# Sums of v in the value tiles of the first group, and its raw x kept as two parts

## The chip, the cores and the metric

The kernel runs on one core of one Trainium2 chip. The metric is the device time of one execution in microseconds (us). The engines are TensorE (PE, its weight loads PEld), VectorE (DVE), ScalarE (ACT), GpSimd (POOL) and SyncE (SP); SP issues all the transfers (DMA) of this program.

## The reference

The input is q, k and v of 4 batches, 8 heads, 768 positions and 64 features. Each position attends to the keys closer than 16 and, besides, to 24 summaries, one for each block of 32 positions. The output of the attention goes through a feed-forward layer with softplus.

```python
k_sum = k.reshape(B, H, nb, block, D).max(axis=3)
v_sum = v.reshape(B, H, nb, block, D).mean(axis=3)
scores_l = scale * np.matmul(q, k.transpose(0, 1, 3, 2))
scores_s = scale * np.einsum('bhsd,bhnd->bhsn', q, k_sum) + np.log(block)
scores_all = np.concatenate([np.where(mask_l, scores_l, -1e9), scores_s], axis=-1)
...
v_all = np.concatenate([v, v_sum], axis=2)
attn = np.matmul(a, v_all)            # a: softmax of scores_all
...
h = x @ w_in                          # x: attn, heads side by side, 3072 x 512
g = np.maximum(h, 0.0) + np.log1p(np.exp(-np.abs(h)))
return g @ w_out                      # 512 x 2048 and 2048 x 512
```

## The kernel before

The 3072 tokens are 12 chunks of 256, and two chunks make a group: x = 0 to 5. A window is 64 queries with 96 keys (KW) and the 24 summaries behind them, so 120 in all (KS). The attention of one chunk works on two head pairs (hp, hp + 1) at once: a block. Each group thus has four blocks, (chunk 0 or 1) by (head pairs 0, 1 or 2, 3).

The feed-forward layer is done twice over: for each group the first half of the 16 slices of the hidden layer, then, from the last group back to group 0, the second half. The second half needs x once more, in another form (a Strassen-like scheme with sums and differences of the four blocks). For that the raw blocks r (128 x 512) of groups 0 to 4 are stored to DRAM at the start (`keep`, DRAM tiles `raw`) and loaded back in the last phases (`attended`). The order of all instructions is a list of task numbers, SEQUENCE, written out in the file; every engine runs its tasks in that order, and so does SP with its DMAs. A tile with `bufs=1` is only written again when its readers are done.

Every x is held as two parts in the PE's rounded format: `xw[:, part 0]` is the rounded value (`high`, L786 on ACT) and part 1 the rest (`low`, L790 on DVE).

Group 0 is treated apart, since the program starts with it:

- `FirstPlaces` puts its queries and values into tiles named `first` (one for each head pair). A value tile has 96 rows for each window; the rows 96 to 119 stay unused.
- `declare_first_values` computes the 24 sums of v on the PE (L430, into `vt`); ACT scales them into `v0` (L441, `mean`), in the rows 96 to 119 of its tile.
- `attention` has the scores on the PE (L646, `sc`), the mask on DVE (L659), the exponential on ACT (L667), the transposes on the PE (L700, `pt`), their copies on ACT (L704, `pT`), and then `values` (L746 and L754, `xo`): 16 matmuls with 96 rows for each block, and for the sums 4 more with 24 rows and 256 columns that add to the same `xo`.
- After that, `take` copies `xo` into a raw block r (L767: two of the four on ACT, two on DVE), which `keep` stores.

In all other groups the sums lie in the rows 96 to 119 of the value tile itself (a DMA spreads them, L545, `v<-vs`), and a value matmul has 120 rows.

Of the kernel before, what the change touches and what calls it, by code (L numbers as in the profile page):

```python
# [10 lines left out]
F32 = mybir.dt.float32  # L11
# [136 lines left out]
23 124 0 125 2 3 25 4 44 47 5 134 161 6 7 24 8 31 27 9 10 126 130 35 11 127 12 128 13 129 14 26 131 33 50 1 132 133a  # L148
51 15 16 52 17 85 18 135 136 66 19 137 20 138 29 21 22 45 82 162 139 37 163 166 53 32 164 54b 165 39 41 67 167 34 284
48 143 68 36 28 55 30 140 57 88 46 168 69 38 49 89 70 40 56 58 90 104 86 180 169 42 84 141a 105 142a 43 106 291 91 59  # L150
309 148a 92a 144 145 146 83 87 147 152 107 170 71 61 108 171 63 62 73 72 292 74 75 334 338 293 149 64 60a 181 93 182
95 183 316 77 79 184 94 96 97 351 76 80 150a 185 120 199 78 294 295a 153a 109 157 154 111 155 110 156 112 113 296 317
158 101 99 100 176 102 151a 159 218 336 115 117 160a 318 297 342 340 116 227 346 98a 118 186 285 121 335 219 339 228
172 173 174 220 319 358 221 229 222 230 223 376 289 337a 114 320b 234 235 224 175 344 286 204 231 177 298 301 299 290
321 241 343 236 287 300 242 187 237 178 341a 225 243 244 226 179 232 288 322 345 359 189 360 233 123 122 239 190 238
245 347 200a 188 302 310 361 383 201 362b 323 348 314 202 240 248 203 468b 472a 205 363 312 313 249 246 303 469b 467
384 326 324 191a 385 325 315 311 255 195a 206a 192 207 364 208 209 256 193 386 194 247 250 251 257 475 252 196 258 327
494b 259 387b 498a 262 349a 365 368 366 263 352 355 328 350 493 356 197a 269 388 367 198a 210a 270 476 353 357 354 495
253 264 211 389 65 643 265 212 214 213 254 271 266 501 272 215 273 369 519 477 260 377 380 216a 217 378 381 261 520a
478 526 521b 390 393 267 370 307 479a 305 308a 306a 372 392 391 382 480 268 373a 329 379 274 502 481 641 278 645 503  # L160
276 330a 332a 333a 277 275 529 394 547 331 548a 549 374a 375 395 399 482 485 484 470 279 397a 398 400 401 402 504 473
483 103 471 474 505 410 403 404 554a 281 282 405 644 506 411 406 412 413 530 507 407 649 647 408 414 409 531 557 486
659a 660b 417 532 533a 418 534 508 509 415 419 648 558 487a 420 510 511 496 500 658 653 304 497 416 421 499 559 655
535 422 642 650 646 665 651 652 424 560 425 561a 426 668 686 427 428 512 513 522 525 536 81 431 438 432 423 429 430
562 669 524 539 537 527 654 517 670 518a 489a 687 693a 523 528 538 563 439 433 440 434 435 441 442 688b 436 671 672b
696 715a 714 119 540 541a 491a 545 550 556 564 566 543a 492a 490a 673 697 719 716 567 552 565 445 446 447 448 437 443
449 656 553 551 555 698 444 396 371 674 450 544 722 741a 742a 699 700a 568 452 569 675 661 573 574 453 515 571a 280
572a 701 546a 516a 575 454 455 283 663 740 745a 576 451 577 578 456 458 488 723 457 459 678 676 657 460 461a 584 585
464a 890 462 724 579 662 580 702 667 677 591 725 726 748 570 586 581 727 833b 582 894 592 587 588 598 749 839 832 664
# [41 lines left out]
1763 1767 1765a 1611 1901 1623 1768 1615 1676 1769a 1677 1678 1620 1616 1679 1680 1682 1685 1770a 1681 1683 1621 1687  # L211
1689 1617 1686 1688 1777a 1766a 1895 1691 1618 1692 1667 1690 1684 1696 1693 1624 1697 1668 1669 1698 1701 1704 1625
1702a 1670 1705 1707 1774a 1708 1712 1703 1713 1710 1706 1711 1714 1716 1674 1709 1715 1717 1721 1675 1898 1694 1780
1718 1905 1722 1723 1726 1622 1729 1727 1728 1735 1732 1730 1695 1737 1626 1731 1736 1778a 1772 1896 1699 1739 1779a
1897a 1733 1775 1781a 1740 1738 1734 1741 1742 1700 1719 1720 1724 1899a 1743 1782a 1773a 1746 1747 1748 1776 1783
1785 1786 1789 1784a 1787 1725 1790 1788 1794 1792 1791 1793 1902a 1795 1796 1757 1797 1744 1745 1798 1799 1800 1805
1806 1750 1807 1751 1810 1811 1758 1753 1755 1812 1819 1813 1820 1814 1749 1754 1756 1815 1752 1821 1816 1823 1817
1822 1818 1759 1825 1826 1908a 1824 1827 1830 1831 1801 1903 1802 1803 1832 1804 1808 1835 1841 1836a 1838 1837 1839
1840 1842 1844 1846 1843 1845 1847 1850 1809 1904 1848 1849 1828 1851 1852 1855 1829 1856 1857 1860 1863 1900a 1866
1862 1911 1861a 1864 1867 1871 1865 1869 1872 1870 1760 1909a 1912 1914a 1913a 1875 1876 1873 1906 1868 1833 1874  # L220
1910a 1877 1834 1915 1853 1880 1916a 1907a 1881 1882 1917 1920 1918a 1919 1923 1921 1928 1926 1922 1887 1891 1930 1854
# [10 lines left out]
def kernel(  # L232
# [9 lines left out]
    nc = tc.nc  # L242
# [233 lines left out]
    class Places:  # L476


        def __init__(self, c, hp, sums, pads, apart):
# [9 lines left out]
            self.apart, self.sums = apart, None  # L489
# [60 lines left out]
    class FirstPlaces:  # L550


        def __init__(self, hp, sums, own, sp):
# [27 lines left out]
            v_keys.append(sums.first_v)  # L581
            self.tiles = []
            for i in range(n_c):
# [4 lines left out]
                tiles.sums = lambda g: sums.first(hp + g)  # L588
# [33 lines left out]
    def attention(x, i, hp, tiles, by_pe):  # L622
# [117 lines left out]
        def values():  # L740
            apart = bool(tiles.sums)
            for g in range(NG):
                for w in range(NWIN):
                    v = tiles.v(g)[:KW if apart else KS, w]
                    for h in range(2):
                        nc.tensor.matmul(  # L746
                            xo()[h * D:(h + 1) * D, g * CH + w * QW:g * CH + (w + 1) * QW],
                            lhsT=v[:, h * D:(h + 1) * D], rhs=queries(g, w, h)[:KW if apart else KS],
                            start=not (apart and (g or w)), stop=not apart,
                        )  # L750
# [9 lines left out]
        order.add(PE, 1.6 if tiles.sums else 1.2, values, [pT, *((pT, k) for k in range(NSQ)), *tiles.v_keys], [xo])  # L760

        r = None
        if x < NX - 1:
            r = block(2 * i + hp // NG)

            def take(copy):
                copy(out=r(), in_=xo())  # L767
            order.add(
                ACT, act(NG * CH, True), lambda: take(nc.scalar.copy), [xo], [r],
                ways=[Way(DVE, dve(NG * CH), lambda: take(nc.vector.tensor_copy))],  # L770
            )
            if x:
                return r
# [18 lines left out]
        return r  # L792
# [509 lines left out]
    for hp in range(0, NHP, NG):  # L1302
# [94 lines left out]
```

## Time and profile before

| | us |
|---|---|
| median of 3 runs (614.16 to 617.19) | 614.34 |
| the profiled execution, its own time | 613.83 |
| its span, first to last instruction | 612.0 |
| PE busy in the span | 602.7 |
| DVE, ACT, POOL busy | 379.3, 343.3, 180.6 |
| granted PE clock, mean | 1.000 |

The rows of the next section are of the profiled execution, whose own time is 613.83 us: its span of 612.0 us and 1.8 us around it. PE is busy for 98% of the span; this is a mean over stages, and what sets the end in a stage is read from the waits of that stage. A line number is that of the kernel before.

### The profile page before, as it was taken

How to read it: one execution, taken by the hardware profiler on the slowest of the kernel's cores; microseconds unless marked ns; L12 is line 12 of the kernel's file. 1: busy time of each engine (PE TensorE's matmuls, PEld its weight loads, DVE VectorE, ACT ScalarE, POOL GpSimd, SP SyncE). 2: the span in 40 equal slices, each digit the busy share in tenths (PEclk: the TensorE clock that was granted, in tenths of full speed). 3: DMA queues.
4: the chain of work that ended last, by engine and by line, in shares of the span. 5: the costliest groups of instructions: out<-in, count | busy, mean ns of one | idle time of the engine just before them, and what ended most of it. 6: DMA issues, size and time to landing. Idle time of an engine off the chain costs nothing.

```text
span 612.0 us, 12214 instructions
## 1 busy us (share of the span) xinstructions
PE 602.7 (98%) x4575; PEld 505.6 (83%) x4575; DVE 379.3 (62%) x992; ACT 343.3 (56%) x846; POOL 180.6 (30%) x178
## 2 busy tenths in 40 slices
PE   8899999999999999999999999999999999999997
PEld 7567878888788888888888888899898989999996
DVE  4999987846465665442235689854765655554543
ACT  4989998986778656576266986432213222233211
POOL 4445255134115132210003553572411216012000
PEclk9999999999999999999999999999999999999999
DMA  8999778966868576665428520041040230020121
GB/s 304 310 314 250 236 238 258 280 193 230 263 196 263 175 213 225 213 201 193 135 75 270 206 70 1 1 155 52 2 172 2 103 138 1 35 103 1 48 92 69
DMA packets 66714, 96.13 MB, mean 157 GB/s; under 512 B 5888, under 2 KB 44896, under 8 KB 65888
## 3 DMA queue, kind: packets, MB, share of 16 engines
q1 hardware_dynamic: 66656, 95.36, 48.1%
q8 instruction: 36, 0.59, 0.4%
q14 instruction: 22, 0.18, 0.1%
HBM read 66.06 MB, written 27.26 MB: 152 GB/s over the span
## 4 chain that ended last, share of the span: by engine, by line
PE 86%; DVE 11%; ACT 2%; issue 1%; POOL 0%; DVEq 0%; ACTq 0%; POOLq 0%
PE po L1224 40%; PE ph L1059 21%; PE hx L1099 10%; PE hy L1099 7%; PE xo L746 4%; PE sc L646 3%; DVE sp L659 1%; PE warm L1298 1%; DVE t L948 1%; DVE t L940 1%; DVE ks L352 1%; DVE w L973 1%; DVE gl L1217 1%; DVE tb L713 1%; DVE t L944 1%
## 5 line engine op out<-in xcount | busy, mean ns | idle before, releaser
L1224 PE MATMUL po<-w,gh 128*128 128x512 f32 x766 | 202.7, 392 | 0.3 <-DVE w L973 0.3
L1224 PEld LDWEIGHTS po<-w,gh 128*128 128x128 f32 x766 | 141.0, 188 | 29.6 <-DVE w L973 0.7
L1059 PE MATMUL ph<-xw,w 128*128 128x512 f32 x672 | 161.9, 392 | 0.2 <-POOL w L973 0.2
L1059 PEld LDWEIGHTS ph<-xw,w 128*128 128x128 f32 x672 | 125.1, 188 | 28.1 <-POOL w L973 0.7
L1224 PE MATMUL po<-w,gl 128*128 128x512 f32 x383 | 114.5, 392 | 0.6 <-DVE gl L1217 0.6
L1224 PEld LDWEIGHTS po<-w,gl 128*128 128x128 f32 x383 | 70.7, 188 | 15.3 <-DVE gl L1217 1.0
L667 ACT ACTIVATE sp<-sp,nm 128x120 f32<-128x120 f32 x192 | 73.1, 384 | 5.9 <-DVE nm L659 5.7
L1209 ACT ACTIVATE gh<-hx 128x512 fp32r<-128x512 f32 x20 | 12.0, 600 | 107.6 <-DVE hx L1109 107.6
L962 POOL TENSOR_TENSOR t<-t,raw 128x1024 int32<-128x1024 int32 (+1 forms) x20 | 40.8, 2044 | 103.9 <-DVE t L948 70.0
L1217 DVE TENSOR_TENSOR gl<-ph,gh 128x512 fp32r<-128x512 f32 x56 | 38.2, 686 | 53.0 <-ACT ph L1213 52.8
L1209 ACT ACTIVATE gh<-ph 128x512 fp32r<-128x512 f32 x56 | 33.4, 598 | 37.7 <-PE ph L1059 37.3
L803 POOL TENSOR_TENSOR x<-r,x 128x512 fp32r<-128x512 f32 x23 | 30.5, 1339 | 67.9 <-DVE x L796 58.2
L659 DVE CUSTOM_DVE_ANT_0 sp<-sc,added 128x120 f32<-128x120 f32 x192 | 40.8, 278 | 5.9 <-PE sc L646 4.9
L667 ACT ACTIVATION_READ_ACCUMULATOR sp<-sp,nm 128x1 f32 x192 | 36.2, 189 | 0.0
L1099 PE MATMUL hx<-x,w 128*128 128x256 f32 x240 | 35.7, 285 | 0.0
L1099 PE MATMUL hx<-x,sw 128*128 128x256 f32 x240 | 35.5, 284 | 0.0
L1099 PEld LDWEIGHTS hx<-x,w 128*128 128x128 f32 x240 | 32.9, 190 | 2.1
L1099 PE MATMUL hy<-x,sw 128*128 128x256 f32 x240 | 34.4, 284 | 0.0
L1209 ACT ACT_TABLE_LOAD x23 | 29.5, 1283 | 6.3 <-PE ph L1059 5.9
L1213 ACT ACTIVATE ph<-ph 128x512 f32<-128x512 f32 x56 | 32.9, 591 | 0.0
L1099 PEld LDWEIGHTS hx<-x,sw 128*128 128x128 f32 x240 | 32.0, 190 | 0.8
L1099 PEld LDWEIGHTS hy<-x,sw 128*128 128x128 f32 x240 | 31.2, 191 | 0.2
(122 smaller groups left out, 828.0 us busy)
## 6 DMA issues: line engine op xcount, KB each, us to landing
squares<-tb SPq DMA_DIRECT2D x20, 512.0 KB
pT<-squares SPq DMA_DIRECT2D x80, 128.0 KB
raw<-w_out_dram SPq DMA_DIRECT2D x16, 512.0 KB
kf<-kT_dram SPq DMA_DIRECT2D x16, 384.0 KB
raw<-w_in_dram SPq DMA_DIRECT2D x6, 1024.0 KB
q<-qT_dram SPq DMA_DIRECT2D x20, 256.0 KB
raw<-r SPq DMA_DIRECT2D x20, 256.0 KB
part<-ob SPq DMA_DIRECT2D x10, 512.0 KB
```

What stands on the lines that cost most here:

```text
L646: nc.tensor.matmul(unit(g * NU + h * NPAIR + i)[r * QW:(r + 1) * QW, k0:k1], lhsT=q[rows, w * QW:(w + 1) * QW], rhs=k[rows], start=True, s ...
L659: nc.vector.tensor_tensor_reduce(out=sp()[:, n], in0=unit(n), in1=added()[:, kinds.index((lows[w], lows[w + 1]))], scale=-SCALE, scalar=FL ...
L667: nc.scalar.activation(sp()[:, n], sp()[:, n], AF.Exp, bias=nm()[:, n:n + 1], scale=-1.0, accum_out=ss()[:, n:n + 1],)
L746: nc.tensor.matmul(xo()[h * D:(h + 1) * D, g * CH + w * QW:g * CH + (w + 1) * QW], lhsT=v[:, h * D:(h + 1) * D], rhs=queries(g, w, h)[:KW ...
L803: engine.tensor_tensor(to(1), a(), to(0).bitcast(F32), op=ALU.subtract)
L962: nc.gpsimd.tensor_tensor(a, a, word(0, I32), op=ALU.add)
L1059: nc.tensor.matmul(ph(), lhsT=lhs(part, cc), rhs=xw[cc][0]()[:, xw[cc][1], a], start=cc == 0 and n == 0, stop=cc == NCC - 1 and n == 2,)
L1099: nc.tensor.matmul(to()[:, half], lhsT=lhs(wa, cc), rhs=of_x(xa)[:, cc * CH:(cc + 1) * CH], start=cc == 0 and m == 0, stop=cc == NG - 1 an ...
L1209: nc.scalar.activation(gh(), all_of(), AF.Softplus)
L1213: nc.scalar.activation(all_of(), all_of(), AF.Softplus)
L1217: nc.vector.tensor_sub(out=gl(), in0=all_of(), in1=gh().bitcast(F32))
L1224: nc.tensor.matmul((to or po[t])()[:, c0:c1], lhsT=a()[:, t * P:(t + 1) * P], rhs=w2()[:, part, i2 * DM + c0:i2 * DM + c1], start=(f == f0 ...
```

## The change

Three things change, all for group 0.

1. The sums of v go into the value tiles: four DMAs (L585 of the changed kernel, one for each head pair) copy the 24 rows of `v0` into the rows 96 to 119 of the `first` tile, once for each of its 8 windows, 96 KiB a DMA. The value matmuls then have 120 rows, and the 4 matmuls for the sums of each block are gone.
2. The raw block r of group 0 is no longer copied out of `xo` and stored. In its place `keep_parts` stores both parts of `xw` (four DMAs of 512 KiB, DRAM tiles `parts`, SBUF to DRAM). In the last phase `summed` loads the two parts of a block into a tile `both` (two DMAs of 256 KiB for a block, where there was one of 256 KiB) and adds them on POOL into r. `both` lies in the places of `tb` and `pT`.
3. SEQUENCE is renumbered; the new tasks stand at chosen places in it, the old ones in the order that they had.

```diff
-23 124 0 125 2 3 25 4 44 47 5 134 161 6 7 24 8 31 27 9 10 126 130 35 11 127 12 128 13 129 14 26 131 33 50 1 132 133a
+23 124 0 125 2 3 25 4 44 48 5 134 161 6 7 24 8 31 27 9 10 126 130 35 11 127 12 128 13 129 14 26 131 33 52 1 132 133a
...
-            v_keys.append(sums.first_v)
+                v_keys.append((own[g], "sums"))
+
+                def load_sums(g=g):
+                    src = sums.first(hp + g).rearrange("n (o c) -> n o c", o=1)
+                    nc.sync.dma_start(out=v(g)[KW:], in_=src.broadcast_to([NB, n_w, P]))
+                order.add(SP, 0.4, load_sums, [sums.first_v], [v_keys[-1]], size=96 * KiB, row=512)
...
-                    v = tiles.v(g)[:KW if apart else KS, w]
+                    v = tiles.v(g)[:, w]
...
-            for g in range(NG if apart else 0):
-                for h in range(2):
-                    c0 = (g * NU + h * NPAIR) * P
-                    nc.tensor.matmul(
-                        xo()[h * D:(h + 1) * D, g * CH:(g + 1) * CH],
-                        lhsT=tiles.sums(g)[:, h * D:(h + 1) * D], rhs=pT()[KW:KS, c0:c0 + NPAIR * P],
-                        start=False, stop=g == NG - 1,
-                    )
...
-        if x < NX - 1:
+        order.add(PE, 1.2, values, [pT, *((pT, k) for k in range(NSQ)), *tiles.v_keys], [xo])
+
+        if 0 < x < NX - 1:
             r = block(2 * i + hp // NG)
...
+    first_parts = {}
+
+    def keep_parts(cc):
+
+        buf, i = whole_x(0)[cc]
+        first_parts[cc] = to = buffer([P, 2, CT], F32, f"parts{cc}", pool=dram, bufs=1)
+        order.add(
+            SP, 0, lambda: nc.sync.dma_start(out=to(), in_=buf()[:, i].bitcast(F32)),
+            [(buf, i, part, k) for part in range(2) for k in range(2)], [to], size=512 * KiB, row=4096,
+        )
+
+    def summed(n, r):
+        i, hp = n // 2, n % 2 * NG
+        both = buffer([P, 2, NG, CH], F32, "both", ("tb", "pT")[n % 2], 1, work)
+        for g in range(NG):
+            def load(g=g):
+                src = first_parts[hp + g]()
+                nc.sync.dma_start(out=both()[:, :, g], in_=src[:, :, i * CH:(i + 1) * CH])
+            order.add(SP, 0, load, [first_parts[hp + g]], [(both, g)], size=256 * KiB, row=1024)
+
+        def add(engine):
+            to = r().rearrange("p (g c) -> p g c", g=NG)
+            engine.tensor_tensor(to, both()[:, 0], both()[:, 1], op=ALU.add)
+        order.add(
+            POOL, pool(NG * CH), lambda: add(nc.gpsimd), [(both, g) for g in range(NG)], [r],
+            ways=[Way(DVE, dve(NG * CH), lambda: add(nc.vector), port=True)],
+        )
...
-            n = 2 * i + hp // NG
-            keep(0, n, attention(0, i, hp, tiles, True))
+            attention(0, i, hp, tiles, True)
+        for cc in range(hp, hp + NG):
+            keep_parts(cc)
```

The order on SP, some 23 to 34 us into the program, where the values of the first group are loaded. Before:

```order
L579 DMA first_232<-v_hp_dram 96x128
L919 DMA raw_444<-w_in_dram 128x2048
L579 DMA first_280<-v_hp_dram 96x7x128
L505 DMA q_528<-qT_dram 128x512
L579 DMA first_280<-v_hp_dram 96x128
L579 DMA first_232<-v_hp_dram 96x7x128
L912 DMA raw_539<-w_out_dram 128x1024
```

and with the change:

```order
L579 DMA first_232<-v_hp_dram 96x128
L937 DMA raw_444<-w_in_dram 128x2048
L579 DMA first_280<-v_hp_dram 96x7x128
L585 DMA first_132<-v0_461 24x8x128
L585 DMA first_134<-v0_461 24x8x128
L585 DMA first_280<-v0_461 24x8x128
L585 DMA first_232<-v0_461 24x8x128
L505 DMA q_528<-qT_dram 128x512
L579 DMA first_280<-v_hp_dram 96x128
L579 DMA first_232<-v_hp_dram 96x7x128
L930 DMA raw_539<-w_out_dram 128x1024
```

The four new DMAs stand together, ahead of the queries q of group 1, of the last two value loads and of the weights.

The order on PE around the values of the first two blocks (`xo` from 29 us on). Before:

```order
L746 MATMUL xo_507<-pT_398,first_132 64x64 x8
L746 MATMUL xo_507<-pT_398,first_134 64x64 x8
L754 MATMUL xo_507<-pT_398,v0_461 64x256 x4
L700 MATMUL pt_545<-ident_81,sp0_210 120x128 x4
L700 MATMUL pt_557<-ident_81,sp0_210 120x128 x4
L746 MATMUL xo_574<-pT_562,first_132 64x64 x8
```

and with the change:

```order
L749 MATMUL xo_511<-pT_398,first_132 64x64 x8
L749 MATMUL xo_511<-pT_398,first_134 64x64 x8
L704 MATMUL pt_545<-ident_81,sp0_210 120x128 x4
L704 MATMUL pt_557<-ident_81,sp0_210 120x128 x4
L749 MATMUL xo_574<-pT_562,first_132 64x64 x8
```

The matmuls on `v0` are gone, and nothing else has moved: the first `xo` now needs what the new DMAs bring into `first_132` and `first_134`.

The order on DVE behind the first block's second `low`. Before:

```order
L790 TENSOR_TENSOR xw_554<-xo_507,xw_554 128x256
L767 COPY r_609<-xo_507 128x512
L933 TENSOR_SCALAR t_611<-raw_444 128x1024
L940 TENSOR_SCALAR t_611<-t_611 128x1024
L944 TENSOR_SCALAR t_611<-t_611 128x1024
```

and with the change:

```order
L781 TENSOR_TENSOR xw_554<-xo_511,xw_554 128x256
L951 TENSOR_SCALAR t_605<-raw_444 128x1024
L958 TENSOR_SCALAR t_605<-t_605 128x1024
L962 TENSOR_SCALAR t_605<-t_605 128x1024
L966 SCALAR_TENSOR_TENSOR t_605<-raw_444,t_605 128x1024
```

The copy into r is gone; the other one on DVE, some 12 us later, likewise.

## Rows read from the trace of the kernel before

**Rows 1.** Waits of PE from 53 us to the end: total, times, longest.
```profile
PE xo L746 <- DVE gl L1217: 0.6, 1, 0.6
PE po L1224 <- DVE w L973: 0.3, 1, 0.3
```

**Rows 2.** The chain that ended last, 27 to 79 us: start, us, what.
```profile
29.23 1.08 PE xo L746 x32
30.31 1.03 PE xo L754 x8
31.36 0.66 ACT xw L786 x2
...
34.42 0.60 DVE r L767
...
46.38 0.60 DVE r L767
...
77.81 1.15 PE xo L746 x32
```

**Rows 3.** Tile v: the PE's sum matmuls and SP's issues of the later spreads (ns).
```profile
L754 PE MATMUL xo<-pT,v x32: 374/374/425, 30.2 to 42.6; 24*64 24x256 f32 x32
...
L545 SPq DMA_DIRECT2D v<-vs x15: 812/817/862, 51.2 to 138.0; - x15
```

**Rows 4.** Timeline of ACT at 27 us: start, us, instruction.
```profile
27.18 0.59 ACT L441 ACTIVATE v<-vt 24x512 f32<-24x512 f32 x1
```

**Rows 5.** Timeline of SP: start, us, issue.
```profile
22.82 0.43 SPq L579 DMA_DIRECT2D first<-v_hp_dram  x1
29.27 0.35 SPq L505 DMA_DIRECT2D q<-qT_dram  x1
...
41.50 0.34 SPq L376 DMA_DIRECT2D st<-v_hp_dram  x1
```

**Rows 6.** Windows 28 to 32 us; the last two columns are DMA share and GB/s.
```profile
28.00:30.00 2.00, 2.00 (x92) 1.97 (x92) 1.97 (x5) 2.00 (x12) 0.00 (x0) 1.00 0.95 234
30.00:31.50 1.50, 1.50 (x22) 0.89 (x17) 1.43 (x4) 1.06 (x7) 0.00 (x0) 1.00 0.77 223
31.50:32.00 0.50, 0.50 (x7) 0.50 (x6) 0.21 (x2) 0.50 (x3) 0.11 (x1) 1.00 0.23 66
```

**Rows 7.** Timeline of SP and of DVE, 0 to 5 us: the first load.
```profile
0.75 0.39 SPq L405 DMA_DIRECT2D kf<-kT_dram  x1
...
3.77 0.95 DVE L352 TENSOR_REDUCE ks<-kf 128x24 f32<-128x768 f32 x1 [3.77 <-DMA kf<-kT_dram]
```

**Rows 8.** Windows 33 to 66 us, columns: PE, PEld, DVE, ACT, POOL busy, clock, DMA, GB/s.
```profile
33.00:53.00 20.00, 18.77 (x290) 13.74 (x286) 19.48 (x59) 18.85 (x59) 8.15 (x6) 1.00 1.00 313
53.00:66.00 13.00, 13.00 (x104) 10.64 (x107) 12.86 (x31) 11.89 (x30) 6.54 (x5) 1.00 0.75 232
```

**Rows 9.** Timeline of DVE and of PE: users of transfers issued in that stretch.
```profile
51.87 1.14 DVE L382 TENSOR_TENSOR st<-st 96x512 f32<-96x512 f32 x2
...
64.50 1.15 PE L746 MATMUL xo<-pT,v 120*64 120x64 f32 x32
```

**Rows 10.** Timeline of POOL, SP and DVE, 489 to 530 us.
```profile
490.34 1.30 POOL L812 TENSOR_TENSOR r<-r 128x512 f32<-128x512 f32 x1
510.19 2.54 POOL L803 TENSOR_TENSOR x<-r,x 128x512 fp32r<-128x512 f32 x2 [18.55 <-DVE x L796]
...
489.00 5.14 SPq L1251 DMA_DIRECT2D out_dram<-ob  x2
...
527.33 1.29 DVE L1261 TENSOR_TENSOR ob<-po,ob 128x512 f32<-128x512 f32 x2 [0.99 <-PE po L1224]
```

**Rows 11.** Windows of the first matmuls (PE busy and its count lead the columns).
```profile
2.00:4.00 2.00, 2.00 (x6) 1.60 (x5) 0.23 (x1) 0.03 (x1) 1.63 (x7) 1.00 0.83 261
8.00:9.00 1.00, 1.00 (x6) 0.90 (x5) 1.00 (x2) 0.00 (x0) 0.60 (x1) 1.00 1.10 427
```

**Rows 12.** Timeline of PE: its longest wait between 10 and 612 us.
```profile
27.86 0.42 PE L646 MATMUL sc<-kf,q 64*64 64x96 f32 x8 [0.90 <-PE vt L430]
```

More of the change, by code (lines that the diff above doesn't have):

```diff
@@ L153 @@
[L153 to L157, printed above, removed]
@@ new lines @@
+106 291 93 61 309 148a 94a 144 145 146 83 88 147 152 107 170 71 62 108 171 64 63 73 72 292 74 75 334 338 293 149 65
+181 95 182 97 183 316 76 78 184 96 98 99 351 79 81 150a 185 120 199 77 80 294 295a 153a 109 157 154 111 155 110 156
+112 113 296 317 158 102 100 101 176 103 151a 159 218 336 114 116 160a 318 297 342 340 115 118 227 346 117 119 186 285
+121 335 219 339 228 172 173 174 220 319 358 221 229 222 230 223 376 289 337a 320b 234 235 224 175 344 286 204 231 177
+298 301 299 290 321 241 343 236 287 300 242 187 237 178 341a 225 243 244 226 179 232 288 322 345 359 189 360 233 123
@@ new lines @@
+122 239 190 238 245 347 200a 188 302 310 361 383 201 362b 323 348 314 202 240 248 203 468b 472a 205 363 312 313 249
+246 303 469b 467 384 326 324 191a 385 325 315 311 255 195a 206a 192 207 364 208 209 256 193 386 194 247 250 251 257
+475 252 196 258 327 494b 259 387b 498a 262 349a 365 368 366 263 352 355 328 350 493 356 197a 269 388 367 198a 210a 270
+476 353 357 354 495 253 264 211 389 643 265 212 214 213 254 271 266 501 272 215 273 369 519 477 260 377 380 216a 217
+378 381 261 520a 478 526 521b 390 393 267 370 307 479a 305 308a 306a 372 392 391 382 480 268 373a 329 379 274 502 481
@@ new lines @@
+641 278 645 503 276 330a 332a 333a 277 275 529 394 547 331 548a 549 374a 375 395 399 482 485 484 470 279 397a 398 400
+401 402 504 473 483 471 474 505 410 403 404 554a 281 282 405 644 506 411 406 412 413 530 507 407 649 647 408 414 409
+531 557 486 659a 660b 417 532 533a 418 534 508 509 415 419 648 558 487a 420 510 511 496 500 658 653 304 497 416 421
+499 559 655 535 422 642 650 646 665 651 652 424 560 425 561a 426 668 686 427 428 512 513 522 525 536 431 438 432 423
+429 430 562 669 524 539 537 527 654 517 670 518a 489a 687 693a 523 528 538 563 439 433 440 434 435 441 442 688b 436
@@ new lines @@
+1675 1900 1901 1694 1902 1780 1718 1911 1912 1722 1913 1723 1726 1622 1729 1727 1728 1735 1732 1730 1695 1737 1626
+1731 1736 1778a 1772 1898 1699 1739 1779a 1899a 1733 1775 1781a 1740 1738 1734 1741 1742 1700 1719 1720 1724 1903a
+1743 1782a 1773a 1746 1747 1748 1776 1783 1785 1786 1789 1784a 1787 1725 1790 1788 1794 1792 1791 1793 1908a 1795 1796
+1757 1797 1744 1745 1798 1799 1800 1805 1806 1750 1807 1751 1810 1811 1758 1753 1755 1812 1819 1813 1820 1814 1749
+1754 1756 1815 1752 1821 1816 1823 1817 1822 1818 1759 1825 1826 1916a 1824 1827 1830 1831 1801 1909 1802 1803 1832
@@ L488, in __init__ @@
             self.q_keys, self.sp_key = [q], (pads, 0)
-            self.apart, self.sums = apart, None
+            self.apart = apart
             self.v_keys = []
@@ L587, in __init__ @@
                 tiles.v = lambda g, w0=w0: v(g)[:, w0:w0 + NWIN]
-                tiles.sums = lambda g: sums.first(hp + g)
                 c0 = i * NG * NU * KS
@@ L747, in values @@
                             xo()[h * D:(h + 1) * D, g * CH + w * QW:g * CH + (w + 1) * QW],
-                            lhsT=v[:, h * D:(h + 1) * D], rhs=queries(g, w, h)[:KW if apart else KS],
-                            start=not (apart and (g or w)), stop=not apart,
-                        )
-            for g in range(NG if apart else 0):
-                for h in range(2):
-                    c0 = (g * NU + h * NPAIR) * P
-                    nc.tensor.matmul(
-                        xo()[h * D:(h + 1) * D, g * CH:(g + 1) * CH],
-                        lhsT=tiles.sums(g)[:, h * D:(h + 1) * D], rhs=pT()[KW:KS, c0:c0 + NPAIR * P],
-                        start=False, stop=g == NG - 1,
-                    )
-        order.add(PE, 1.6 if tiles.sums else 1.2, values, [pT, *((pT, k) for k in range(NSQ)), *tiles.v_keys], [xo])
-        r = None
-        if x < NX - 1:
+                            lhsT=v[:, h * D:(h + 1) * D], rhs=queries(g, w, h), start=True, stop=True,
+                        )
+        order.add(PE, 1.2, values, [pT, *((pT, k) for k in range(NSQ)), *tiles.v_keys], [xo])
+        if 0 < x < NX - 1:
             r = block(2 * i + hp // NG)
@@ L1336, in attended, with load @@
             r[n] = block(n)
-            def load(n=n):
-                nc.sync.dma_start(out=r[n](), in_=kept(x, n)())
-            order.add(SP, 0, load, [kept(x, n)], [r[n]], size=256 * KiB, row=2048)
+            if x:
+                def load(n=n):
+                    nc.sync.dma_start(out=r[n](), in_=kept(x, n)())
+                order.add(SP, 0, load, [kept(x, n)], [r[n]], size=256 * KiB, row=2048)
+            else:
+                summed(n, r[n])
             prepare(x, n, r)
```

54 lines of the change are left out of this document (18 added, 36 removed), and 12 rows, old and new, of the table SEQUENCE.

## The prediction, made before the changed kernel ran

> **What bounds the kernel now.** I read the waits of the PE first. Behind 53 us it waits twice, for 0.9 us together [rows 1], so whatever reaches the PE late at the start stays in the time, and whatever comes earlier is gained in full. What sets the start is then in the chain that ended last. It runs through the first value matmuls: `xo` at 29.23, the four sum matmuls at 30.31, done at 31.34; then ACT's `high` at 31.36, and from there DVE alone, one instruction behind the other, until the PE's `xo` at 77.81 [rows 2]. So between 31 and 78 us the bound is DVE, although the page has it busy for 62% of the span. A change at the start counts by what it does to the end of the first `xo` and by what it takes off DVE in this stretch; PE work that is saved elsewhere in it counts nothing.
>
> **What the change takes off the chain.** The sum matmuls of the first block: 1.03 us, and the two copies into r that fell to DVE: 0.60 and 0.60 [rows 2]. Together 2.23 us. The other three sets of sum matmuls (8 records of 374 ns each, one behind the other in about 1.0 us [rows 3]) and the two copies on ACT stand beside DVE's chain, not in it, and I count them at nothing: DVE would cover up to 3 us of PE work there. The value matmuls now have 120 rows in place of 96. Before, 32 records with 96 rows take 1.08 us, and 32 with 120 rows take 1.15 with the end of the last one [rows 2]; nothing again.
>
> **What it adds: a wait for the spread sums.** Before, the sums were ready for the PE when ACT had scaled them, at 27.18 + 0.59 = 27.77 [rows 4], before `xo` began. Now SP wakes at 27.8 and issues four DMAs. Later DMAs of the same kind, from SBUF to SBUF, take 0.82 us of SP each [rows 3], so they go out until 31.1. The first `xo` needs the first two. SP issued nothing between 23.25 and 29.27 [rows 5], and still the DMA engines are at a share of 0.95 from 28 to 30 us: they work off a queue. The share is 0.77 until 31.5, and 0.23 only after that [rows 6]. The bytes tell how long the old queue is: 0.47 MB from 28 to 30 and 0.33 MB to 31.5, 0.80 MB in all. At most 0.31 MB of it were issued after 29.27 (q, 256 KiB, and a value load of 48 KiB). So at least 0.49 MB were old, 2.1 us at 234 GB/s: on the mean the old queue ends at 30.1. A transfer lands when its last part does, and the last engines are still at it until 31.5. I take that later end, since the queue is there in the rows: 31.5, 0.4 for 96 KiB at 234 GB/s, 0.1 to wake the PE: `xo` begins at 32.0, not at 29.23. The second tile lands 0.4 later, just ahead of the second half of the matmuls.
>
> The Trainium skill, page "DMA: Bandwidth & Descriptors", speaks on both sides. Its section "Queues, rings and completion order" says that on each DMA engine descriptors are consumed in ring order, by which the spread sums stand behind all of the old queue, as I take it. Its section "Anatomy of one DMA" (a fit for the GpSimd path) has about 2.0 us plus the bytes at 436 GB/s; the estimate by it is 2.2 us for 96 KiB, hence 30.0, `xo` done at 31.1 and the sum at -1.4 us. The one load that met an empty queue, the first of the program, agrees with that formula (2.9 us for 384 KiB against the 3.0 measured); the question is only whether the queue is empty, and [rows 6] say no.
>
> Bounds of this wait: from below, the first load of the program was used 3.0 us after its issue on an empty queue [rows 7], so 30.8; from above, all four spreads, q and the small load ahead of the PE's wake, 0.7 MB behind 30.1 at 234 GB/s, 33.1, and 0.4 for uneven engines, 33.5.
>
> **The sum.** `xo` done at 32.0 + 1.08 = 33.1 in place of 31.34: +1.75. The two copies: -1.20. Together +0.55 us: 613.83 becomes 614.4. With the bounds: 30.8 gives -0.7, 33.5 gives +2.05. The median before is 614.34, 0.5 above the profiled execution, and so I put 614.9 as the time that will be measured.
>
> **What hides the rest.** On SP the four issues hold back what stands behind them: q of group 1 (29.27, now 31.1), two value loads, then weights; these the PE wants only after two blocks, two rounds of transposes and a set of scores. Then come the parts. They are 2.1 MB of stores, in a stretch where the DMA share is 1.00 with 313 GB/s [rows 8]; the stores that they replace stand later in SP's order. Two of them (1.05 MB, 3.35 us) go ahead of the load `st`, issued at 41.50 [rows 5], which DVE uses at 51.87 [rows 9]: 10.4 us. `parts1` also lets SP wait for the last `low` of its head pair, some 1.5 us. That leaves 10.4 + 0.55 - 1.5 - 3.35 = 6.1 us, and the queue of 23.25 to 29.27 shows that a load can take 6. The cover is just used up. For the PE's `xo` at 64.50 [rows 9] all four parts (6.7 us) count; from 53 to 66 the share is 0.75 [rows 8], which gives 3.3 us back. I take nothing, with 0 to 2 us as bounds.
>
> At the end, four adds of the form of `r<-r`, 1.30 us each, go to POOL, in its order right ahead of 490.34; POOL then had nothing to do for 18.55 us, until 510.19 [rows 10]. Blocks 0 and 2 share the tile `tb`, 1 and 3 `pT`, so two pairs of loads wait for an add: 5.2 us of adds, 1.3 for the instruction among them and twice about 3.9 (two issues and the 3.0 of [rows 7]) from 490.3 make 504.6, before 510.19. SP stands still meanwhile, and the stores of 489.00 and the loads of `ob` behind them come 10 us later; DVE reads those at 527.33 [rows 10]. Nothing; without the cover, some 1 us.
>
> **The rivals.**
>
> - *The spread sums land early.* For it: DMA engines that have run dry by 30.1 on the mean. Against it: the share of 0.77 until 31.5. Time: 30.8 gives 614.34 - 0.7 = 613.6; on the skill's figure above 612.9.
> - *The stores of the parts are not hidden*: slower. DVE stands at `st` or the PE at the `xo` of 64.50 and all behind them waits. It decides from the point at which the queue costs a load more than 6.1 us. Taken at 2 us: 616.9.
> - *The PE's clock falls*: slower. At the start the same matmul is done six times from 2 to 4 us, and six times from 8 to 9 [rows 11]: the lower and the higher level (1.2 and 2.4 GHz), although the column has 1.00 in both; ahead of the rise the engine had worked without a break. The longest wait behind that, 0.90 us, did not lower it [rows 12]. Now the PE would stand from 29.23 to 32.0, 2.8 us. From 33 to 53 us it is busy for 18.77 of 20 [rows 8], so some 4 us at half the rate would cost about 3 that nothing covers: 617.9. The Trainium skill, page "TensorE: Matmul & The Clock Gate", section "Part 1: The HAM clock gate", has "the default state is throttled, and activity releases the throttle"; no row here shows what a wait of 2.8 us does.
> - *The last phase waits for an add*: +1, 615.9.
>
> **How the numbers follow.** The forecast has 0.57, early landing 0.13, the parts 0.17, the clock 0.10, the last phase 0.03. Half a per cent, 3.07 us, is about what a measurement of this kernel can tell from no change. Faster by more would take 611.3; the chain can give 2.23 us even without any wait, so only what I have overlooked is left: 0.03. Slower by more begins at 617.4: the clock's 0.10, the upper end of the parts, 0.04, and some for both together, 0.02: 0.16. The rest, 0.81, is no change that can be told. The forecast's own range is 613.6 to 616.4; down to 612.9 it takes in the early landing, up to 618.0 the parts and the clock.
>
> **What the profile of the changed kernel would show.** The PE's first `xo` begins at about 32.0, with a wait of some 2.8 us ahead of it whose releaser is the transfer into `first`; a beginning below 31.5 speaks for early landing, one above 33 for the upper bound. The chain then still runs through ACT's `high` and DVE to a PE `xo` at about 78.4, with no r in it. DVE shows no wait for a DMA at `st`, and the PE none ahead of its `xo` at about 65. The count of matmuls from 33 to 53 us shows whether the clock held. In the last phase POOL's four adds end before 506, and no PE wait has grown. Wrong I would be, above all, if the parts fill the queue more than I reckon, or if DVE is not what sets 33 to 78 us once the PE comes late.

## The result: 0.9% slower, and outside the range

The changed kernel takes 619.48 us (median of 11 runs, 617.48 to 622.78), the kernel before 614.23 (11 runs, 613.47 to 617.19) beside it; the ratio is 1.0092, interval 1.0079 to 1.0105. Forecast were 614.9 us and a range up to 618.0. The profiled execution took 619.48, with a span of 617.7 against 612.0.

The page of the profile after: span, and busy time, share and instructions of each engine.

```profile
span 617.7 us, 12156 instructions
...
PE 600.7 (97%) x4543; PEld 505.1 (82%) x4543; DVE 381.3 (62%) x990; ACT 343.0 (56%) x844; POOL 186.3 (30%) x182
```

The PE has 2.0 us less work and ends 5.7 later. Where it stood shows in its timeline, the value matmuls of group 0 and the first three of group 1 (start, us, instruction, the wait ahead of it).

```profile
33.19 1.97 PE L749 MATMUL xo<-pT,first 120*64 120x64 f32 x32 [4.42 <-issue]
...
36.99 1.43 PE L749 MATMUL xo<-pT,first 120*64 120x64 f32 x32
...
41.77 1.17 PE L749 MATMUL xo<-pT,first 120*64 120x64 f32 x32 [1.02 <-ACT pT L708]
...
44.91 1.17 PE L749 MATMUL xo<-pT,first 120*64 120x64 f32 x32 [0.95 <-ACT pT L708]
...
68.20 1.15 PE L749 MATMUL xo<-pT,v 120*64 120x64 f32 x32 [0.55 <-DMA pT<-squares]
...
81.25 1.15 PE L749 MATMUL xo<-pT,v 120*64 120x64 f32 x32 [0.33 <-DVE gl L1235]
...
103.39 1.15 PE L749 MATMUL xo<-pT,v 120*64 120x64 f32 x32
```

The first `xo` begins at 33.19 in place of 29.2 [rows 2], after a wait of 4.42 us that the forecast had at 2.8, and it takes 1.97 us, not 1.15. The releaser is given as "issue": the profile's views show nothing that the PE waits for, though the instruction needs the spread sums. SP, the windows and the trace's records of the semaphores say what it was. A transfer lands in pieces, and each piece raises the transfer's semaphore when it is there. The pieces of the first spread land from 30.51 to 33.10 us, and the first `xo` begins 0.09 behind the last one (the second spread, which it needs from its second half on, is complete at 33.35). The same 0.09 lies between the two in `sums_only`, `ahead`, `sums_ahead`, `half_spread`, `late_stores` and `queue_pool`. SP's issues after:

```profile
27.33 3.54 SPq L585 DMA_DIRECT2D first<-v  x4
30.97 0.81 SPq L505 DMA_DIRECT2D q<-qT_dram  x1
```

Windows of the same stretch; behind the busy times stand the granted clock, the DMA share and GB/s.

```profile
29.00:30.00 1.00, 0.00 (x0) 0.00 (x0) 0.93 (x3) 1.00 (x7) 0.00 (x0) 1.00 1.05 183
30.00:31.00 1.00, 0.00 (x0) 0.00 (x0) 0.97 (x3) 0.47 (x3) 0.00 (x0) 0.72 0.90 205
31.00:32.00 1.00, 0.00 (x0) 0.00 (x0) 0.25 (x2) 0.00 (x0) 0.57 (x1) 0.50 0.79 170
32.00:33.00 1.00, 0.00 (x0) 0.00 (x0) 0.00 (x0) 0.00 (x0) 1.00 (x1) 0.50 0.74 192
33.00:34.00 1.00, 0.81 (x16) 0.84 (x17) 0.00 (x0) 0.00 (x0) 1.00 (x2) 0.50 0.99 255
34.00:36.00 2.00, 2.00 (x27) 1.88 (x24) 0.12 (x1) 0.65 (x2) 0.47 (x1) 0.50 1.11 256
36.00:38.00 2.00, 2.00 (x29) 1.57 (x30) 2.00 (x18) 1.49 (x5) 0.00 (x0) 0.68 1.00 337
```

The DMA engines stay busy longer than before [rows 6], and while the PE stands still its granted clock goes from 1.00 to 0.50, from the higher level (2.4 GHz) to the lower (1.2). It is up again between 36 and 38 us. From 37 to 45 us the chain that ended last runs through ACT, not DVE (start, us, what):

```profile
37.58 1.48 ACT sp L671 x7
```

Later the chain runs through two transfers that were not in it before (start, us, what), and DVE and ACT wait for them:

```profile
45.64 9.84 DMA st<-v_hp_dram
...
79.27 6.96 DMA raw<-w_out_dram
```

```profile
55.50 1.14 DVE L382 TENSOR_TENSOR st<-st 96x512 f32<-96x512 f32 x2 [0.56 <-DMA st<-v_hp_dram]
```

```profile
86.33 1.28 ACT L954 ACT_TABLE_LOAD   x1 [1.43 <-DMA raw<-w_out_dram]
87.62 1.14 ACT L954 ACTIVATE t<-raw 128x1024 f32<-128x1024 f32 x1
```

The reason is seen in SP's own waits from 38 to 62 us (what it waited for: total, times, longest). Before, SP waited for no landing in this stretch; its five waits there, up to 3.0 us, were for the PE, DVE and ACT.

```profile
SPq L791 <- DMA raw<-w_in_dram: 2.0, 1, 2.0
...
SPq L527 <- DMA parts<-xw: 1.6, 2, 0.8
...
SPq L729 <- DMA parts<-xw: 0.9, 1, 0.9
SPq L729 <- DMA kf<-kT_dram: 0.7, 1, 0.7
```

These waits are for no data. SP's issues take eight semaphores in turn, and each waits until the transfer that had its semaphore before, eight issues earlier, has landed: DMAHW7, for one, stands in rows 31, 39 and 47 of SP's order.

```
31 L579 DMA first<-v_hp_dram 96x128 [waits DMAHW7_49]
39 L791 DMA parts_678<-xw 128x1024 [waits DMAHW7_49,DVE_49]
47 L791 DMA parts_779<-xw 128x1024 [waits DMAHW7_49,DVE_49]
```

In the last phase the adds lie where they were put, and the PE has no wait between 480 and 618 us:

```profile
495.98 1.31 POOL L806 TENSOR_TENSOR r<-both 128x512 f32<-128x512 f32 x1
502.47 1.28 POOL L806 TENSOR_TENSOR r<-both 128x512 f32<-128x512 f32 x1 [5.18 <-DMA both<-parts]
...
504.94 1.31 POOL L806 TENSOR_TENSOR r<-both 128x512 f32<-128x512 f32 x1
510.70 1.28 POOL L806 TENSOR_TENSOR r<-both 128x512 f32<-128x512 f32 x1 [4.45 <-DMA both<-parts]
515.80 2.54 POOL L821 TENSOR_TENSOR x<-r,x 128x512 fp32r<-128x512 f32 x2 [3.81 <-DVE x L814]
```

### The profile page after: what moved, and what is told of

It reads as the page before. It is cut to its first block, busy times and chain, and to the rows that moved or that the text cites. A ratio compares the mean times of both kernels' runs of the same rounds, so it can differ in the third digit from the quotient of the medians.

```text
span 617.7 us, 12156 instructions
## 1 busy us (share of the span) xinstructions
PE 600.7 (97%) x4543; PEld 505.1 (82%) x4543; DVE 381.3 (62%) x990; ACT 343.0 (56%) x844; POOL 186.3 (30%) x182
## 4 chain that ended last, share of the span: by engine, by line
PE 76%; DVE 10%; ACT 7%; DMA 4%; issue 2%; POOL 1%; SPq 0%; DVEq 0%; ACTq 0%; POOLq 0%
PE po L1242 36%; PE ph L1077 16%; PE hx L1117 9%; PE hy L1117 7%; PE xo L749 3%; PE sc L650 3%; DMA raw<-w_out_dram 2%; DVE sp L663 2%; DMA st<-v_hp_dram 2%; PE warm L1316 1%; ACT sp L671 1%; ACT raw L972 1%; DVE ks L352 1%; DVE w L991 1%; POOL t L980 1%
## 6 DMA issues: line engine op xcount, KB each, us to landing
squares<-tb SPq DMA_DIRECT2D x20, 512.0 KB
raw<-w_out_dram SPq DMA_DIRECT2D x16, 512.0 KB
part<-ob SPq DMA_DIRECT2D x10, 512.0 KB
out_dram<-ob SPq DMA_DIRECT2D x10, 512.0 KB
```

## The experiments

All times are medians beside runs of the kernel before on the same chip (614.2 to 614.5). The table has the starts of four `xo` on the PE in the profiled execution of each kernel, as the lag behind the kernel before (there 29.16, 40.78, 77.81 and 98.89), and the lag of the span. A profiled execution can stand off its median: those of `sums_only` (621.28), `parts_only` (617.72) and `late_stores` (625.20) are the slowest runs of their kernels.

| kernel | us | ratio, interval | first | 4th | 77.81 | 98.89 | span |
|---|---|---|---|---|---|---|---|
| changed | 619.48 | 1.0092 [1.0079, 1.0105] | +4.0 | +4.1 | +3.4 | +4.5 | +5.7 |
| sums_only | 619.93 | 1.0089 [1.0072, 1.0106] | +5.3 | +5.9 | +5.9 | +6.0 | +7.5 |
| parts_only | 615.22 | 1.0017 [1.0001, 1.0032] | 0.0 | -0.2 | +1.0 | +2.7 | +3.9 |
| late_stores | 621.95 | 1.0136 [1.0104, 1.0167] | +5.6 | +5.7 | +4.7 | +4.7 | +11.1 |
| kept_busy | 619.29 | 1.0087 [1.0066, 1.0107] | +4.5 | +3.2 | +3.6 | +4.8 | +5.7 |
| sums_busy | 618.44 | 1.0062 [1.0041, 1.0084] | +6.0 | +5.3 | +5.4 | +5.4 | +6.5 |
| ahead | 618.93 | 1.0080 [1.0050, 1.0109] | +2.6 | +1.9 | +3.6 | +3.4 | +4.5 |
| sums_ahead | 617.41 | 1.0041 [1.0024, 1.0059] | +2.8 | +2.8 | +2.8 | +3.5 | +4.6 |
| half_spread | 618.53 | 1.0063 [1.0040, 1.0086] | +2.5 | +4.6 | +4.1 | +4.1 | +4.7 |
| queue_pool | 621.89 | 1.0120 [1.0096, 1.0144] | +6.4 | +6.9 | +7.0 | +7.1 | +8.8 |
| no_stores | 613.73 | 0.9987 [0.9973, 1.0000] | -0.9 | -1.0 | -1.2 | -1.5 | -1.5 |
| stores_pool | 614.62 | 1.0007 [0.9997, 1.0018] | -0.1 | -0.3 | -1.2 | -1.4 | -0.6 |
| pool_r | 617.71 | 1.0049 [1.0031, 1.0066] | -0.7 | -0.3 | +2.3 | +2.3 | +4.5 |

### Each part alone, and later stores

`sums_only`: the changed kernel with r of group 0 copied and kept as before.

```diff
-            attention(0, i, hp, tiles, True)
-        for cc in range(hp, hp + NG):
-            keep_parts(cc)
+            n = 2 * i + hp // NG
+            keep(0, n, attention(0, i, hp, tiles, True))
```

> The kernel before with the first part of the change alone: the sums of v are spread by the four DMAs into the value tiles, the raw block r is copied and stored as before. Theory A (the wait for the spread sums and the lower clock behind it reach the end): with the whole change the first xo was done at 35.18 us in place of 31.34, 3.84 later; DVE is the bound behind it and keeps both of its copies, so the time is 614.2 + 3.8 = 618.0, with the first xo at about 33.2 and the matmuls behind it at half rate. Theory B (the start has room for the late xo, and the stores of the parts make the whole loss): about 614.2.

619.93: the sums make the whole loss. The first `xo` came 5.3 us late, later than in the changed kernel's profile though the program is the same up to there. From the second `xo` on the lag stays within 0.4 us as far as 206 us: a late start is passed on in full. (What the table's +7.5 has beyond that comes behind it, 1.3 us of it from a wait of the PE for another transfer at 218 us.) That is theory A; its 3.8 was too small since the wait was.

`parts_only`: the sum matmuls back, the rest of the change kept.

```diff
-                    v = tiles.v(g)[:, w]
+                    v = tiles.v(g)[:KW if apart else KS, w]
```

> The kernel before with the second part of the change alone: the sum matmuls and v0 as before, but r of group 0 neither copied nor stored; the two parts of x are stored where the whole change stores them, and added in the last phase. Theory A (the four stores of 512 KiB hold up the loads behind them): DVE saves 1.2 us of copies and loses it again at st and at the weights of w_out, 1 to 3 us: 614 to 616, with a wait of SP for a landing between 40 and 64 us, and a DVE wait at st. Theory B (the stores are hidden, all loss comes from the spread sums): 614.2 - 1.2 = 613.0.

615.22: theory A. The chain has the late transfers (start, us, what), and ACT stands still for the last one:

```profile
55.10 7.07 DMA st<-v_hp_dram
...
65.57 5.72 DMA raw<-w_out_dram
...
76.95 7.50 DMA raw<-w_out_dram
```

```profile
84.54 1.28 ACT L961 ACT_TABLE_LOAD   x1 [2.09 <-DMA raw<-w_out_dram]
85.83 1.12 ACT L961 ACTIVATE t<-raw 128x1024 f32<-128x1024 f32 x1
```

SP waited from 40 to 60 us for landings, as forecast there; at `st` DVE lost less than expected, the loss comes with the w_out weights, used at 85.83. Before:

```profile
82.79 1.15 ACT L936 ACTIVATE t<-raw 128x1024 f32<-128x1024 f32 x1
```

`late_stores`: the four stores at 90, 99, 112 and 124 us.

```diff
-L791 DMA parts_678<-xw 128x1024
 L937 DMA raw<-w_in_dram 128x2048
-L791 DMA parts_688<-xw 128x1024
 L376 DMA st<-v_hp_dram 96x1024
```

> The whole change, with the four stores of the parts moved in SP's order from 41 to 53 us to about 88, 98, 108 and 118 us, where the old kernel stored r. Theory A (the stores cost about 1 us at st, 1 us at the w_out weights around 86 us and 0.5 to 1 behind that): 619.4 - 2.5 = 616.9, and no DVE wait at st. Theory B (the stores cost nothing, the late start makes the loss): 619.4.

621.95, a miss for both theories. To 104 us it went as theory A has it (lag falling from 5.7 to 4.7). But these places, from 90 us on, are no better; behind the third store the PE waits twice within one block:

```profile
115.20 0.68 PE L749 MATMUL xo<-pT,v 120*64 120x64 f32 x16 [1.07 <-DMA pT<-squares]
116.96 0.69 PE L749 MATMUL xo<-pT,v 120*64 120x64 f32 x16 [1.08 <-DMA v<-vs]
```

### What the clock costs

`kept_busy`: the changed kernel with 11 matmuls (22 records) on the identity in the wait; `sums_busy`: the same in `sums_only`.

```diff
+    for _ in range(11):
+        def once_more():
+            wide = ident().rearrange("p (o c) -> p o c", o=1).broadcast_to([P, 2, P])
+            nc.tensor.matmul(still(), lhsT=ident(), rhs=wide, start=True, stop=True)
+        order.add(PE, 0.6, once_more, [ident], [still])
```

> The whole change, and 11 matmuls on the identity, whose result nobody reads, on the PE between the scores of the second block and the first xo, about 0.37 us each, so that the engine works through the wait for the spread sums. Theory A (the clock fell because PE stood still, and the fall costs time): the first xo takes 1.15 us in place of 1.97, the transposes and the second xo behind it 0.3 less each, and the time is 619.4 - 1.3 = 618.1. Theory B (what comes late is bound by ACT and DVE, so the clock costs nothing): 619.4. If the clock falls for another reason than the wait, xo still takes 1.97.

> The spread sums alone (r copied and stored as before), and the 11 idle matmuls on the identity ahead of the first xo, as in kept_busy. There the clock held and the four blocks came 1.2 us nearer together, but by 100 us the loads of w_out had taken that back. Here no stores of the parts stand ahead of those loads. Theory A (the clock costs about 1.2 us where nothing else is late): 619.9 - 1.2 = 618.7, and the lag of the xo at 78 us falls by 1.2 against its own first xo. Theory B (the clock costs nothing here either): 619.9.

The clock held in both (mean 1.000 and 0.999): standing still in the wait had lowered it. In `kept_busy` the lag falls by 1.3 us to the fourth block, where the changed kernel's grows by 0.1. Yet the time is the same, as far as intervals of about 1 us can tell. ACT's step on the last w_out weights begins with the landing of their load, 0.3 us later than in the changed kernel:

```profile
86.64 1.28 ACT L955 ACT_TABLE_LOAD   x1 [1.56 <-DMA raw<-w_out_dram]
```

In `sums_busy` nothing stands in the way there, ACT does not wait, and the 618.44 against 619.93 are 1.5 us, close to the 1.2 of theory A. The intervals of the two ratios overlap, so the times alone do not show it; the lags (0.8 down against 0.6 up to the fourth block), each of one execution, speak for it.

### What the spread sums wait for

`ahead`: the changed kernel with the 1 MB load of weights behind the first two spreads; `sums_ahead`: the same in `sums_only`.

```diff
-L937 DMA raw<-w_in_dram 128x2048
-L585 DMA first<-v_461 24x8x128 x4
+L585 DMA first<-v_459 24x8x128 x2
+L937 DMA raw<-w_in_dram 128x2048
+L585 DMA first<-v_459 24x8x128 x2
```

> The whole change with one load of SP moved: the 1 MB load of w_in weights (raw_444, issued at 22.0 us) goes behind the first two of the four spreads, so that it no longer stands ahead of them. Theory A (the spreads stand behind all loads issued before them; 1 MB is 3.4 us at the 300 GB/s of this stretch): the first xo begins at about 30 in place of 33.2 and the time is 619.5 - 3.2 = 616.3. Theory B (a spread is slow by itself, since 24 rows are read 8 times in pieces of 512 B): the first xo stays at 33 and the time at 619.5. Theory C (DVE needs the moved weights as soon as it has the first parts of x, at 35 us before): xo is early, but DVE waits for raw_444 and the time stays above 618.

> The spread sums alone (r copied and stored as before), with the same 1 MB load moved behind the first two spreads. Theory A: the first xo at about 30, no later than 0.8 behind the kernel before, its end not later than the end of the old sum matmuls: 614.2 within 1 us, in place of 619.9. Theory B: 619.9. Theory C: above 618, with DVE waiting for the weights.

`xo` came at 31.78 and 31.94: the queue does cost, 1.4 to 2.5 us of it, but not all. The windows of `ahead` show that with the load gone the queue was empty, and its timelines of SP and PE how late the `xo` still is:

```profile
28.00:29.00 1.00, 0.98 (x57) 0.87 (x48) 1.00 (x2) 1.00 (x7) 0.00 (x0) 1.00 0.00 0
29.00:30.00 1.00, 0.00 (x0) 0.00 (x0) 0.95 (x3) 1.00 (x7) 0.00 (x0) 1.00 0.49 107
```

```profile
27.55 1.89 SPq L585 DMA_DIRECT2D first<-v  x2
```

```profile
31.78 1.15 PE L749 MATMUL xo<-pT,first 120*64 120x64 f32 x32 [2.81 <-issue]
```

From 28 to 29 us the engines moved nothing, and still the `xo` stood until 4.2 us after the first issue. So A is half right, and something else is left.

`half_spread`: each spread cut in two, those for the first block first; a row then has 4 pieces of 512 B in place of 8.

```diff
+                for i in range(n_c):
+                    def load_sums(g=g, i=i):
...
+                        nc.sync.dma_start(out=v(g)[KW:, i * NWIN:(i + 1) * NWIN], in_=src.broadcast_to([NB, NWIN, P]))
```

> As sums_ahead, with each spread cut in two DMAs of 4 windows (12 pieces of 512 B a row less in each), those for the first block first; the 1 MB load of weights goes behind the first four. The queue ahead is empty as there, where the first spread took 4.1 us from its issue to the first xo. Theory A (a spread's time is bytes: from 29 to 31 us the engines moved only some 100 GB/s, so 96 KiB less for the first block is 1 us): first xo at about 30.9, time 617.4 - 1 = 616.4. Theory B (the time is one fixed latency from the issue, and two issues at 0.9 us): first xo at 31.5 to 31.9 and the time at 617.4.

With half the bytes the wait is the same, 4.2 us from the first issue: the time of theory B, but not a fixed latency. (Eight issues take SP 7.5 us, which pushes the loads behind them back; that may be why the time is no better than that of `sums_ahead`, whose interval it meets.)

```profile
27.46 4.23 SPq L584 DMA_DIRECT2D first<-v  x4
```

```profile
31.62 1.73 PE L749 MATMUL xo<-pT,first 120*64 120x64 f32 x32 [2.74 <-issue]
```

The trace shows one late piece. In `ahead` eleven pieces of the first spread land between 30.02 and 30.27 us, at most 2.7 us behind the issue, and the last at 31.69; in `half_spread` eleven land between 29.63 and 29.77, at most 2.3 us behind it, and the last at 31.53. (The semaphore's first rise, at 28.93 and 28.83, is no landing: the engines had moved nothing.) So half the bytes bring the eleven 0.4 us nearer to their issue, and the last 0.1. In the gap the DMA share is that of one engine in 16 (`ahead`, then `half_spread`):

```profile
30.80:31.40 0.60, 0.00 (x0) 0.00 (x0) 0.57 (x3) 0.00 (x0) 0.00 (x0) 1.00 0.08 15
```

```profile
30.40:31.20 0.80, 0.00 (x0) 0.00 (x0) 0.77 (x3) 0.19 (x2) 0.00 (x0) 1.00 0.07 9
```

What held that engine can be read from the packets. A packet of 16 KB on another DMA queue, of the kind "instruction", begins at 29.07 in `ahead` and takes 1.35 us, until 30.42; in `half_spread` it begins at 29.52 and takes 0.93, until 30.45, and in `sums_ahead` it lasts from 29.02 to 30.50. Right behind it the late share of the first spread begins to move, on one engine, which goes on when the others are done. The packets carry no engine's number here, so that it is the same engine is inferred from the times, and no run moved this packet.

`queue_pool`: the spreads of `sums_only` on POOL's queue.

```diff
-                    nc.sync.dma_start(out=v(g)[KW:], in_=src.broadcast_to([NB, n_w, P]))
+                    nc.gpsimd.dma_start(out=v(g)[KW:], in_=src.broadcast_to([NB, n_w, P]))
```

> The spread sums alone, with the four spreads issued by POOL, which has nothing to do there, through its own queue in place of SP's; all the rest as in that kernel (SP's later loads go out up to 3.5 us earlier). Theory A (a transfer waits for what stands ahead of it in its own queue): the spreads pass by the old loads, the first xo begins at 30 to 31 and the time is 615 to 616. Theory A2 (whichever queue it stands in, a transfer waits for its turn at engines that are busy): xo stays at 33 to 34.5 and the time at about 619.9.

```profile
27.48 2.63 POOL L585 DMA_DIRECT2D first<-v  x4 [0.71 <-ACT v L441]
```

```profile
35.58 1.98 PE L749 MATMUL xo<-pT,first 120*64 120x64 f32 x32 [6.68 <-issue]
```

Another queue passed nothing by; 35.58 is the latest of all, and the pieces of its first spread land from 30.79 to 35.49 us, no earlier than through SP's queue (30.92 to 34.36 in `sums_only`). That is what theory A2 expects. A path of POOL's own that is slower would look alike, since the DMA share is above 1.00 from 28 to 36 us; the run does not tell them apart.

### What the parts cost

`no_stores`, `stores_pool` and `pool_r` start from `parts_only`, `parts_only` and the kernel before.

```diff
-                src = first_parts[hp + g]()
+                src = kT[0, hp + g][:, :2 * CH].rearrange("p (two c) -> p two c", two=2)
...
-        for cc in range(hp, hp + NG):
-            keep_parts(cc)
```

> The second part of the change alone, without the four stores of the parts; the last phase loads keys in place of the parts and adds those, the same number of bytes with the same adds on POOL (so the x of group 0 in the second half is not the right one). Theory A (the stores cost what the saved copies had given): 614.2 - 1.2 = 613.0, and no wait of SP for a landing between 38 and 60 us. Theory B (the saved copies give nothing, or the adds at the end cost): 615.2 as with the stores.

```diff
-            SP, 0, lambda: nc.sync.dma_start(out=to(), in_=buf()[:, i].bitcast(F32)),
+            POOL, 0.7, lambda: nc.gpsimd.dma_start(out=to(), in_=buf()[:, i].bitcast(F32)),
```

> The second part of the change alone (as parts_only: 615.2), with its four stores of 512 KiB issued by POOL, at places where POOL had nothing to do, through POOL's own queue; SP's order is that of the kernel before without the stores of r. The bytes and their times are nearly the same. Theory A (the stores cost because SP stands until earlier transfers have landed, and issues the loads behind them late): without that wait the time is 613.7, as without the stores. Theory B (the 2.1 MB themselves cost, whoever issues them, since the DMA engines are at their limit from 40 to 60 us): 615.2, with the same late st and w_out loads.

`no_stores` is 0.7 us faster than before, `parts_only` 1.0 slower, and the two intervals only just do not meet: the stores cost 1.7. The copies are worth 0.7 in the median, not the 1.2 of their durations, though its interval (nothing to 1.7 us) takes in both; in its profile the lag goes from -0.9 to -1.5. `stores_pool` has the same bytes and lies between, 614.62; its times alone do not tell A from B, its interval meets both. Its trace speaks for A. SP issued the last w_out loads at 73.47 (73.77 before, 76.53 in `parts_only`); ACT had them in time:

```profile
81.70 1.15 ACT L961 ACTIVATE t<-raw 128x1024 f32<-128x1024 f32 x1
```

`pool_r`: is there a way to drop the copies without a store more?

```diff
+        def sum_parts():
+            for g in range(NG):
+                buf, k = xw[hp + g]
+                high, low = (buf()[:, k, part, cols].bitcast(F32) for part in range(2))
+                nc.gpsimd.tensor_tensor(r()[:, g * CH:(g + 1) * CH], high, low, op=ALU.add)
```

> The kernel before with one thing changed: r of group 0 is not copied out of xo by DVE and ACT, but added on POOL from the two parts of x, 2 adds of 128 x 256 a block, and stored as before; no DMA is added or moved. Theory A (without the stores of the parts the saved copies give the 0.7 us that no_stores showed): 613.7 against 614.4. Theory B (POOL's adds share DVE's port or delay the weights that POOL prepares): 614.4 or more.

617.71: theory B. Two adds take 2.34 us on POOL, and while they run DVE's step of 0.70 takes 1.10 (POOL, then DVE, then the same step before):

```profile
34.23 2.34 POOL L799 TENSOR_TENSOR r<-xw 128x256 f32<-128x256 f32 x2
```

```profile
34.88 1.10 DVE L951 TENSOR_SCALAR t<-t 128x1024 f32<-128x1024 f32 x1
```

```profile
35.66 0.70 DVE L940 TENSOR_SCALAR t<-t 128x1024 f32<-128x1024 f32 x1
```

No version beat the kernel before by more than these measurements can tell.

## Why the prediction was wrong

- **What bounds the kernel: right in what counts.** Nothing behind 53 us gives a late start back; in `sums_only` the lag of the second `xo` is there at 206 us. That DVE alone sets 31 to 78 us did not outlast the change: ACT is in the chain from 37 to 45 us, and `st` behind it.
- **The wait for the spread sums: the step that failed.** It put the end of the old queue at 31.5 us, and added 0.4 for 96 KiB and 0.1 to wake the PE: 32.0. The first `xo` began at 33.19, and at 34.45 and 34.77 in two kernels with the same program up to there; the upper bound, 33.5, did not hold. The mechanism was the right one, a transfer lands with its last piece and the last engine sets it; its size was not. With the old queue the last piece came at 33.10 in the changed kernel, 2.6 us behind the first, and at 34.36 and 34.68 in the two others, where the rest had landed by 33.94 and 32.31. With the queue empty it came 1.4 us behind the others (`ahead`), so that the lower bound of 30.8, from a load out of DRAM that met an empty queue [rows 7], was met by eleven pieces and missed by one. The queue adds 1.4 to 3.0 to 31.78. The Trainium skill, page "DMA: Bandwidth & Descriptors", section "Anatomy of one DMA", gave the estimate of 2.2 us for a spread; in the empty queue of `ahead` the eleven pieces had it at 2.5 to 2.7 behind the start of the issue and the last at 4.1, and the measurement decides. Of the ring order, section "Queues, rings and completion order" of the same page, the trace agrees in that taking 1 MB from ahead of the spreads brought them 1.4 and 2.5 us forward (`ahead`, `sums_ahead`); no run here shows the order on one engine.
- **The clock: a rival at 0.10 that came true, with less to pay.** The granted clock fell in the wait, and the first `xo` took 1.97 in place of 1.15. The price was put at 3 us, for some 4 us at the lower level, which no row gave; the windows have some 6 to 7, part of them spent standing still. `sums_busy` gives 1.5 by the medians, within noise, and in the changed kernel no price can be told, since the w_out loads take it back (`kept_busy`).
- **The first `xo` done:** forecast 1.75 us later than before, measured 3.84 (35.18 against 31.34). Of the 2.1 between, 1.2 are the wait and 0.9 the clock.
- **The copies: 1.2 us taken, 0.7 measured** (`no_stores`), with 1.2 inside the interval. The sum matmuls off the chain cannot be seen alone, as the wait took their place.
- **The parts, "the cover is just used up": mis-sized, within its bounds.** Taken at 0, bounds 0 to 2; they cost 1.7 (`parts_only` against `no_stores`). The step looked at `st` and the `xo` of 64.50, where 0.6 and 0.5 us were lost; what it left out are the w_out loads further back in SP's order, which SP issues late because it stands for landings. With the spread sums in front, copies and stores come out even: 1.0092 against 1.0089.
- **The last phase: right.** The last add ends at 512.0, not before 506, and 5.6 of that is the lag of the whole program there; POOL's next instruction then waits another 3.81 us for DVE, and the PE waits for none of it.

In sum: spread sums +5.5 (0.0089 of 614.2), copies -0.7, stores +1.7 make 6.5, against 5.7 measured (0.0092); the 0.8 between lies within the intervals, about 1 us each. Open: why one or two pieces of a spread came up to 2.4 us behind the rest with the queue full (32.31 and 34.68 in `late_stores`), so that the first `xo` began at 33.2 in one execution and at 34.8 in another, and how much of the loss in `parts_only` is SP's standing and how much the bytes.

## What to carry to other kernels

A transfer is there when its last piece is: look at the slowest DMA engine, not at the bytes and their mean rate. Here a small transfer, put in the place of 1 us of matmuls, took 4.2 us from its issue to the PE with nothing of SP's queued ahead, and 5.9 to 7.9 behind a queue (`sums_busy`); ask when its source is ready, before asking how many bytes it moves. A store added in the middle of an in-order queue is paid by loads well behind it: follow the queue until the first load that an engine waits for. And a gain at one stage only counts up to the next thing that comes at its own time; find that one first.

## What the runs showed of the hardware that was not expected

- A spread from SBUF to SBUF, issued with the DMA engines at a share of 0.00, had eleven pieces there 2.5 to 2.7 us after its issue and the last after 4.1 (`ahead`); with half the bytes it was 2.2 to 2.3 and 4.1 (`half_spread`). A 16 KB packet of instructions, 0.93 to 1.48 us long in these runs, ended just before the late piece began to move.
- In `ahead` the PE was back at work at 31.78, after 2.81 us; its clock was 1.00 until 33 us and fell only then, to 0.50, with the PE busy throughout. This is what a wait of 2.8 us does, which no row of before showed; the Trainium skill, page "TensorE: Matmul & The Clock Gate", section "Part 1: The HAM clock gate", has the throttled state as the default, and the fall agrees. A long wait is not the only thing that goes before a fall: in `no_stores` the granted clock was 0.87 from 42 to 43 us and 0.50 from 43 to 44, with no wait of the PE above 0.29 us between 28 and 43.

```profile
32.00:33.00 1.00, 1.00 (x33) 0.93 (x29) 0.00 (x0) 0.03 (x1) 1.00 (x1) 1.00 0.49 197
33.00:34.00 1.00, 1.00 (x6) 1.00 (x6) 0.35 (x2) 0.74 (x3) 1.00 (x2) 0.55 1.00 401
34.00:36.00 2.00, 2.00 (x29) 1.66 (x30) 2.00 (x18) 1.79 (x7) 0.68 (x1) 0.50 1.00 300
```

- Adds on POOL slowed DVE's steps of 0.70 us beside them to 1.10 (`pool_r`).
